# Moving the convolution of nine of 32 feature chunks from TensorE to GpSimd in a fused attention and gated-convolution kernel

## The chip, the cores and the metric

The kernel runs on one core of a Trainium2 chip. The metric is the device time of one execution in microseconds (us). Every run also has a granted TensorE clock, as a share of full speed, and a state: "slow" is a run more than 1.5% above the fastest run of the same kernel. One run of a kernel has no known state.

## The reference, cut to what matters

Attention over sorted blocks (omitted here) gives `x` of 4 batches x 768 positions x 512. The part that the change touches is the gated layer after it:

```python
h = np.maximum(x @ w_in, 0.0)              # 768 x 1024 per batch
hp = zero-padded h, one position at each end
for k in range(3):
    conv_out += conv_w[k][None, None, :] * hp[:, k:k + S, :]   # each feature by itself
gate = 1.0 / (1.0 + np.exp(-conv_out))
return (h * gate @ w_out).astype(np.float32)
```

The 1024 features are eight chunks of 128, one feature per partition; with four batches there are 32 chunks. A chunk's convolution is three taps, each with one weight per feature.

## The kernel before

The program is a list of tokens, `ORDER`, and each token issues a few instructions. All engines take their own instructions in the order in which the tokens stand, so the table is the schedule. A digit after `d` is one of four PSUM slots; a last `a` or `d` chooses ScalarE or VectorE for an eviction.

```python
NET, NHE, NSG, NXN, NOS = 6, 12, 6, 4, 6      # NOS: output buffers
ORDER = """
... S.1.4d3 C.0.5d1 V.1.2d2 R.2.1 E.1.4 K.2.1d0 Ce.0.5 Ve.1.2d H.0.1.1d3 R.2.7 PV.1.3d2 Ge.0.5 ...
"""                                            # cut: 551 tokens in all

def do_R(b, n, eng, slot):                     # GpSimd: one of eight copies for batch b's values
    nc.gpsimd.tensor_copy(rv[:, n * 8:(n + 1) * 8, 0:CC], vr[b]...)

def do_H / do_He                               # cut: first layer on TensorE; hE = 0.5 * relu, bf16

def do_C(b, f, eng, slot):                     # convolution of chunk f on TensorE
    pu = bank(slot, [128, 2, 512])
    def mm(n, x0, nx, tap, src, start=False, stop=False):
        for i in range(2):                     # diagonal 64 x 64 weights, two quadrants
            o = 64 * (1 - i if n else i)
            nc.tensor.matmul(pu[o:o + 64, n, ...], lhsT=dg[64 * i:64 * (i + 1), tap, f, :],
                             rhs=src[64 * i:64 * (i + 1)], ..., tile_position=(64 * i, o))
    mm(...)                                    # eight calls, 16 matmuls

def do_Ce(b, f, eng, slot):                    # ScalarE: tanh of the sum, three instructions
    nc.scalar.activation(sg[:, 0:384], pu[:, 0, 0:384], AF.Tanh)
    for o in (0, 64):
        nc.scalar.activation(sg[o:o + 64, 384:768], pu[64 - o:128 - o, 1, 0:384], AF.Tanh)

def do_Ge(b, f, eng, slot):                    # VectorE: the gate product, hg = (sg + 1) * hE
    nc.vector.scalar_tensor_tensor(out=hg, in0=sg, scalar=1.0, in1=hx[:, :, 0:128],
                                   op0=OP.add, op1=OP.mult)

def do_O / do_Oe                               # cut: second layer, eviction to o_sb{x % NOS}, store
```

The convolution is a product with diagonal weights, so TensorE spends 16 matmuls on work that is one multiply per element and tap. GpSimd is used for loads, for a few set-up products and for the `rv` copies (`do_R`), on which the `V` matmuls of the next batch wait.

The softmax here doesn't subtract the row's maximum and nothing guards it: scores larger than these inputs give would overflow.

## Time and profile before

| | before |
|---|---|
| median of 3 runs | 178.96 us (178.92 to 181.91) |
| TensorE busy, profiled run | 162.9 of 176.1 us (92%), clock 1.0 |
| TensorE weight loads busy | 106.9 us (61%) |
| GpSimd busy | 42.0 us (24%) |
| the 32 gate products on VectorE | 981 ns each |

The lines themselves are in the prediction below, but for that of the gate product:

```profile
L495 DVE SCALAR_TENSOR_TENSOR hg<-sg,hE 128x768 bf16<-128x768 bf16 x32 | 30.8, 981 | 2.7 <-ACT sg L486 2.5
```

A slice digit is the busy share of a fortieth of the span in tenths; the chain's shares say whose work, followed back from the last instruction, the end rested on. In a group line, `x32 | 30.8, 981` is the count, the busy us in all and the mean ns of one; after the next bar come the idle us just before them and what ended them.

### The profile page before, as it was taken

The page shows a single profiled execution, that of the slowest core. Times are in us where ns is not written, and L with a number is a line of the kernel's source. Part 1 is how long each engine was busy: PE and PEld are TensorE (multiplying, and loading weights), DVE is VectorE, ACT ScalarE, POOL GpSimd, SP SyncE. Part 2 cuts the span into 40 slices and gives each one's busy share as a digit, 9 for nine tenths or more (in the row PEclk, how much of TensorE's full clock was granted, in tenths as well). Part 3 has the DMA queues.
Part 4 walks back from the last instruction along what each step waited for, and adds up shares of the span by engine and source line. Part 5 has one row for each costly group of instructions (what it writes and reads, how often), then busy time and mean ns, then how long its engine had stood idle before and what let it go on. Part 6 is the DMA issues. An engine that isn't in the chain of part 4 may idle for free.

```text
span 176.1 us, 6511 instructions
## 1 busy us (share of the span) xinstructions
PE 162.9 (92%) x2907; PEld 106.9 (61%) x2918; DVE 118.4 (67%) x224; ACT 116.7 (66%) x210; POOL 42.0 (24%) x96
## 2 busy tenths in 40 slices
PE   3997989998889999999999999999999999999991
...
POOL 7850940399791001008600000000000000000000
...
GB/s 48 200 212 89 113 219 217 196 220 209 215 200 218 203 110 4 0 7 0 63 60 120 121 92 90 62 61 4 2 4 60 6 0 0 63 119 60 180 181 119
DMA packets 10688, 18.27 MB, mean 104 GB/s; under 512 B 908, under 2 KB 6052, under 8 KB 10660
## 3 DMA queue, kind: packets, MB, share of 16 engines
...
## 4 chain that ended last, share of the span: by engine, by line
PE 69%; ACT 13%; DVE 10%; issue 3%; DMA 3%; DVEq 0%; ACTq 0%
PE D L502 22%; PE D L447 22%; PE D L467 9%; ACT et L402 4%; PE D L413 4%; PE D L333 3%; PE D L367 3%; DVE hE L457 3%; PE D L430 2%; ACT kT L102 2%; ACT hE L455 2%; DMA sn<-in_sort_net_dram 2%; PE D L394 2%; PE D L230 2%; ACT sg L486 2%
## 5 line engine op out<-in xcount | busy, mean ns | idle before, releaser
L447 PE MATMUL D<-xT,w_in_bf 128*128 128x384 bf16 x256 | 46.3, 326 | 0.8 <-DVE hE L457 0.5
L502 PE MATMUL D<-w_out_bf,hg 128*128 128x512 bf16 x181 | 42.7, 379 | 0.6 <-issue 0.2
L447 PEld LDWEIGHTS <-w_in_bf 128*128 128x128 bf16 x256 | 23.6, 98 | 15.4 <-issue 1.3
L495 DVE SCALAR_TENSOR_TENSOR hg<-sg,hE 128x768 bf16<-128x768 bf16 x32 | 30.8, 981 | 2.7 <-ACT sg L486 2.5
L486 ACT ACTIVATE sg<-D 64x384 bf16<-64x384 f32 x64 | 31.1, 486 | 0.8
L502 PEld LDWEIGHTS <-hg 128*128 128x128 bf16 x192 | 17.8, 98 | 20.6 <-issue 0.8
L354 POOL COPY rv<-vr 128x384 bf16<-128x384 bf16 x24 | 20.9, 910 | 36.6 <-PE D L367 25.6
L402 ACT ACTIVATE et<-D 128x768 bf16<-128x768 f32 x32 | 24.3, 820 | 6.6 <-PE D L394 6.6
L457 DVE TENSOR_SCALAR hE<-D 128x384 bf16<-128x384 f32 x29 | 15.7, 554 | 16.2 <-ACT hE L455 9.7
L455 ACT ACTIVATE hE<-D 128x384 bf16<-128x384 f32 x35 | 16.1, 491 | 14.6 <-PE D L447 7.7
L422 DVE TENSOR_TENSOR xn<-D,rc 96x512 bf16<-96x512 f32 x32 | 22.0, 687 | 1.1
L467 PE MATMUL D<-hE,dg 64*64 64x384 bf16 (+2 forms) x512 | 19.6, 286 | 0.7 <-PE D L394 0.5
L484 ACT ACTIVATE sg<-D 128x384 bf16<-128x384 f32 x32 | 15.8, 492 | 4.2 <-PE D L467 3.4
L106 DVE COPY o_sb<-D 128x512 f32<-128x512 f32 x13 | 8.9, 692 | 13.6 <-PE D L502 11.0
L467 PEld LDWEIGHTS <-dg 64*64 64x64 bf16 x512 | 12.5, 106 | 6.6 <-issue 3.6
L102 ACT COPY o_sb<-D 128x512 f32<-128x512 f32 x11 | 6.4, 587 | 13.8 <-PE D L502 13.7
L413 PE MATMUL D<-vE,et 128*128 128x65 bf16 x256 | 13.2, 194 | 0.8 <-ACT hE L455 0.5
L413 PEld LDWEIGHTS <-et 128*128 128x128 bf16 x256 | 10.6, 98 | 4.2 <-issue 2.2
L102 ACT CAST kT<-D 128x1024 bf16<-128x1024 f32 x10 | 9.9, 1013 | 3.5 <-PE D L333 3.3
L394 PE MATMUL D<-qT,kT 64*128 64x96 bf16 x256 | 9.5, 204 | 1.2 <-DVE qT L106 0.3
L420 DVE RECIPROCAL rc<-D 96x8 f32<-96x8 f32 x32 | 6.3, 198 | 6.0 <-PE D L413 5.9
L430 PE MATMUL D<-ident,xn 96*128 96x96 bf16 x128 | 9.9, 206 | 0.3
...
## 6 DMA issues: line engine op xcount, KB each, us to landing
...
w_out_bf<-in_moe_w_out_dram POOLq DMA_DIRECT2D x1, 1024.0 KB, 12.5
...
sn<-in_sort_net_dram SPq DMA_DIRECT2D x1, 8.0 KB, 3.2
```

The lines of the kernel that those rows point to most:

```text
L102: nc.scalar.copy(dst, src)
L354: nc.gpsimd.tensor_copy(rv[:, n * 8:(n + 1) * 8, 0:CC], vr[b].rearrange("p c d -> p d c")[:, n * 8:(n + 1) * 8, :])
L402: nc.scalar.activation(et[:, 0:8 * BLK].rearrange("c (h q) -> c h q", h=2), at.pop(("S", b, j))[:, :, 0:4 * BLK], AF.Exp, scale=scale)
L413: nc.tensor.matmul(pov[:, hh, ii, :], lhsT=et[:, o:o + 128], rhs=vE[b % 2][:, (hh * HP + hp) * NB + sub * 4 + ii, 0:65], start=True, stop= ...
L422: nc.vector.tensor_mul(xn.rearrange("c i h d -> c h i d"), pov[0:BLK, :, :, 0:64], rc.unsqueeze(3).to_broadcast((BLK, 2, 4, D)))
L447: nc.tensor.matmul(ph[:, n, 0:384], lhsT=w_in_bf[:, kc, f * 128:(f + 1) * 128], rhs=xT[(b, s)][:, kc, :], start=(kc == 0), stop=(kc == KC ...
L455: nc.scalar.activation(hv, src, AF.Relu, scale=0.5)
L457: nc.vector.tensor_scalar(hv, in0=src, scalar1=0.0, scalar2=0.5, op0=OP.max, op1=OP.mult)
L467: nc.tensor.matmul(pu[o:o + 64, n, (x0 - 3 * n) * 128:(x0 - 3 * n + nx) * 128], lhsT=dg[64 * i:64 * (i + 1), tap, f, :], rhs=src[64 * i:64 ...
L486: nc.scalar.activation(sg[o:o + 64, 384:768], pu[64 - o:128 - o, 1, 0:384], AF.Tanh)
L495: nc.vector.scalar_tensor_tensor(out=hg.rearrange("p (x c) -> p x c", c=128), in0=sg.rearrange("p (x c) -> p x c", c=128), scalar=1.0, in1 ...
L502: nc.tensor.matmul(po, lhsT=hgs[(b, f)][:, x * 128:(x + 1) * 128], rhs=w_out_bf[:, f, :], start=(f == 0), stop=(f == FC - 1))
```

## The change

Its intent is to take nine convolutions from the nearly full TensorE and to do them on the nearly idle GpSimd, as scaled copies and adds in SBUF with an fp32 sum. ScalarE then needs one tanh instead of three. Two output buffers are given up, presumably for the fp32 tiles, and a new table is used for the whole kernel.

```diff
-NET, NHE, NSG, NXN, NOS = 6, 12, 6, 4, 6
+NET, NHE, NSG, NXN, NOS = 6, 12, 6, 4, 4
+ON_POOL = [(0, 1), (0, 3), (1, 1), (1, 3), (1, 5), (2, 1), (2, 3), (2, 5), (3, 1)]
 ORDER = """
-Q.0.1d0 K.0.2d1 K.0.1d2 Qe.0.1d Ke.0.2a M.0.2d1 ...
+K.0.2d0 Ke.0.2a Q.0.1d1 Qe.0.1d K.0.1d2 bdm.0d3 ...          # cut: the whole table is new
+... C.0.5d3 S.1.5d0 U.0.1.0 PV.1.0d1 Ce.0.5 ... He.0.3.1d U.0.1.1 ...
 """
+    def do_U(b, f, half, eng, slot):
+        g = b * FC + f
+        h = hE[g % NHE]
+        hx = h[:, 2:].rearrange("p (x c) -> p x c", c=130)
+        if half == 0:
+            at[("C", b, f)] = moep.tile([128, NX, 128], FP, name="u", bufs=2)
+            nc.gpsimd.tensor_scalar(at[("C", b, f)], in0=hx[:, :, 0:128], scalar1=cws[:, 1, f:f + 1],
+                                    scalar2=None, op0=OP.mult)
+        u = at[("C", b, f)]
+        a = moep.tile([128, 2 + NX * 130], FP, name="tap", bufs=1)
+        nc.gpsimd.tensor_scalar(a, in0=h, scalar1=cws[:, 2 * half, f:f + 1], scalar2=None, op0=OP.mult)
+        ...                                    # cut: parts = the shifted views of a, 640 and 128 wide
+        for x0, nx, src in parts:
+            nc.gpsimd.tensor_tensor(out=u[:, x0:x0 + nx], in0=u[:, x0:x0 + nx], in1=src, op=OP.add)
     def do_Ce(b, f, eng, slot):
+        if (b, f) in ON_POOL:
+            nc.scalar.activation(sg, pu.rearrange("p x c -> p (x c)"), AF.Tanh)
+            return
```

So a chunk on GpSimd is three scaled copies (one of 768 and two of 782 elements) and four adds (two of 640, two of 128). Below, "chunk" means these seven instructions.

More of the change, by code (lines that the diff above doesn't have):

```diff
@@ L13 @@
 AX = mybir.AxisListType
-NET, NHE, NSG, NXN, NOS = 6, 12, 6, 4, 6
+NET, NHE, NSG, NXN, NOS = 6, 12, 6, 4, 4
+ON_POOL = [(0, 1), (0, 3), (1, 1), (1, 3), (1, 5), (2, 1), (2, 3), (2, 5), (3, 1)]
 SUBS = [(hp, s) for s in range(2) for hp in range(4)]
 ORDER = """
-Q.0.1d0 K.0.2d1 K.0.1d2 Qe.0.1d Ke.0.2a M.0.2d1 M.0.1d0 win.0 M.0.0d3 Ke.0.1d lk.1 bdm.0d2 Me.0.2a Me.0.0a K.0.0d1
-lv.1 lq.1 lk.2 Ke.0.0a Me.0.1d lv.2 bdv.0 V.0.0d0 V.0.1d2 S.0.0d3 S.0.1d1 dg.0.2 Ve.0.0d E.0.0 Ve.0.1d V.0.3d0
-S.0.2d2 E.0.1 V.0.2d3 E.0.2 S.0.3d1 Ve.0.3d S.0.5d0 bd.1 Ve.0.2d bd.3 E.0.3 PV.0.0d3 X.0.0 E.0.5 S.0.6d2 PV.0.1d1
@@ L24 @@
-S.0.7d0 X.0.1 PV.0.2d3 lq.2 E.0.6 T.0.0d2 S.0.4d1 E.0.7 Te.0.0a PV.0.3d0 E.0.4 X.0.2 T.0.1d3 bd.2 PV.0.5d2 Te.0.1a
-T.0.2d1 X.0.3 Te.0.2d T.0.3d0 Te.0.3d PV.0.4d3 X.0.5 PV.0.6d1 H.0.0.0d0 R.1.7 H.0.2.0d2 X.0.4 K.1.1d3 He.0.1.0a
-He.0.0.0d He.0.5.0d He.0.4.0a K.1.2d0 Ke.1.2a X.0.6 Ke.1.1d K.1.0d2 H.0.3.0d1 lk.3 T.0.4d3 Ke.1.0a R.1.1 R.1.6
-T.0.5d0 Te.0.4d PV.0.7d2 R.1.0 He.0.7.0d H.0.1.0d3 He.0.6.0a R.1.2 R.1.3 X.0.7 dg.0.1 T.0.6d1 Te.0.5d He.0.2.0a
-He.0.3.0d Te.0.6d V.1.3d2 V.1.0d0 Ve.1.0a Q.1.1d1 Ve.1.3d Q.1.0d3 lq.3 R.1.5 T.0.7d0 Qe.1.1d Te.0.7a S.1.3d1 Qe.1.0d
@@ L29 @@
-E.1.3 S.1.2d2 dg.0.0 S.1.0d3 E.1.2 S.1.1d0 H.0.2.1d1 S.1.5d2 E.1.1 V.1.1d0 R.1.4 E.1.0 He.0.5.1d He.0.4.1d E.1.5
-Ve.1.1d S.1.4d3 C.0.5d1 V.1.2d2 R.2.1 E.1.4 K.2.1d0 Ce.0.5 Ve.1.2d H.0.1.1d3 R.2.7 PV.1.3d2 Ge.0.5 PV.1.1d1 Ke.2.1a
-X.1.3 He.0.2.1a R.2.0 X.1.1 C.0.2d0 R.2.3 He.0.3.1a H.0.0.1d3 PV.1.0d1 Ce.0.2 T.1.3d2 He.0.0.1d X.1.0 He.0.1.1a
-S.1.7d0 PV.1.2d3 Te.1.3a C.0.1d2 E.1.7 T.1.0d1 Ce.0.1 PV.1.7d0 Te.1.0a X.1.2 H.0.3.1d3 X.1.7 He.0.7.1d He.0.6.1a
-T.1.2d0 Te.1.2d S.1.6d2 E.1.6 Ge.0.1 C.0.3d1 T.1.1d3 PV.1.5d0 Q.2.0d2 Te.1.1a X.1.5 R.2.2 R.2.6 K.2.2d3 Ce.0.3
@@ L34 @@
-Ke.2.2a Q.2.1d0 Qe.2.0d C.0.0d1 C.0.7d2 PV.1.6d3 Qe.2.1d Ce.0.0 H.1.0.0d0 X.1.6 Ce.0.7 T.1.7d1 Te.1.7a H.1.1.0d3
-He.1.0.0d Q.3.1d2 Q.3.0d1 Ge.0.2 He.1.2.0a He.1.3.0a Ge.0.3 He.1.1.0a Qe.3.1d K.2.0d3 T.1.6d0 R.2.5 Ge.0.0 Ke.2.0a
-lv.3 R.2.4 H.1.3.0d2 He.1.7.0a PV.1.4d3 He.1.6.0a Te.1.6d V.2.2d0 Qe.3.0d C.0.4d1 T.1.5d2 X.1.4 H.1.2.0d3 Ve.2.2d
-Ce.0.4 T.1.4d0 Te.1.5d S.2.1d2 C.0.6d1 He.1.4.0d He.1.5.0a S.2.3d3 E.2.1 Te.1.4d K.3.1d0 Ge.0.7 Ce.0.6 E.2.3 wout.0
-H.1.2.1d2 Ke.3.1d S.2.0d1 S.2.2d0 He.1.5.1d E.2.0 H.1.0.1d3 E.2.2 K.3.0d1 He.1.1.1a He.1.4.1d Ge.0.6 He.1.0.1d
@@ L39 @@
-V.2.0d0 V.2.3d3 Ke.3.0a C.1.4d2 Ve.2.3a Ge.0.4 Ce.1.4 Ve.2.0d H.1.1.1d1 K.3.2d3 He.1.3.1a He.1.2.1d V.2.1d0 S.2.4d2
-H.1.3.1d1 Ke.3.2d He.1.7.1d C.1.1d3 E.2.4 Ve.2.1a He.1.6.1a Ce.1.1 C.1.0d2 PV.2.3d0 Ge.1.4 O.0.4d1 Ce.1.0 C.1.5d3
-X.2.3 C.1.3d0 Oe.0.4d Ce.1.5 PV.2.1d1 R.3.5 O.0.1d2 C.1.2d3 Ge.1.1 Ce.1.3 Ce.1.2 X.2.1 Oe.0.1d Ge.1.5 C.1.7d1
-PV.2.0d2 O.0.3d0 X.2.0 O.0.2d2 Ge.1.2 Ce.1.7 Oe.0.3d S.2.5d0 R.3.2 E.2.5 Ge.1.0 S.3.1d1 R.3.4 R.3.3 Oe.0.2d C.1.6d3
-E.3.1 O.0.0d2 Ge.1.3 Ce.1.6 T.2.3d1 Ge.1.7 O.0.5d0 Oe.0.0d R.3.7 Ge.1.6 Te.2.3a PV.2.2d1 R.3.1 T.2.0d2 Oe.0.5a X.2.2
@@ L44 @@
-Te.2.0a O.1.0d3 T.2.1d1 T.2.2d2 V.3.1d0 Oe.1.0a Te.2.2d R.3.0 S.2.7d3 S.2.6d2 Te.2.1a Ve.3.1a O.1.2d1 R.3.6 E.2.6
-O.1.3d0 Oe.1.2d PV.2.4d1 E.2.7 Oe.1.3a V.3.2d3 Ve.3.2a X.2.4 V.3.3d2 PV.2.6d0 X.2.6 H.2.1.0d1 T.2.4d3 Te.2.4d
-Ve.3.3a PV.2.5d0 S.3.4d2 X.2.5 He.2.3.0a V.3.0d3 He.2.2.0a Ve.3.0d S.3.0d1 E.3.4 PV.2.7d0 E.3.0 O.1.5d2 T.2.6d3
-T.2.5d1 X.2.7 Oe.1.5d H.2.0.0d0 Te.2.5d S.3.3d1 S.3.2d2 E.3.2 Te.2.6d O.1.1d3 E.3.3 He.2.0.0a He.2.1.0d T.2.7d2
-Te.2.7d PV.3.0d1 Oe.1.1a S.3.6d0 X.3.0 E.3.6 PV.3.1d2 H.2.1.1d3 S.3.5d0 S.3.7d1 X.3.1 PV.3.3d2 He.2.3.1a E.3.5
@@ L49 @@
-He.2.2.1d H.2.2.1d3 X.3.3 PV.3.2d2 T.3.1d0 E.3.7 H.2.2.0d1 He.2.5.1a X.3.2 Te.3.1a T.3.2d2 He.2.4.1d Te.3.2d T.3.0d0
-C.2.3d3 Te.3.0d PV.3.6d2 T.3.3d0 X.3.6 He.2.5.0a He.2.4.0a Te.3.3d H.2.0.1d1 Ce.2.3 T.3.6d2 He.2.1.1a PV.3.7d0
-He.2.0.1d C.2.5d3 Te.3.6a X.3.7 C.2.2d1 PV.3.5d2 Ce.2.5 H.2.3.0d0 X.3.5 He.2.6.0d C.2.0d2 He.2.7.0d Ce.2.2 C.2.1d3
-PV.3.4d1 Ce.2.0 Ge.2.3 Ge.2.2 O.1.4d0 H.3.1.0d2 X.3.4 Ce.2.1 Oe.1.4a T.3.4d3 T.3.7d0 Ge.2.0 Te.3.4d He.3.3.0d
-He.3.2.0a H.3.0.0d1 H.2.3.1d2 T.3.5d3 Te.3.7d Ge.2.1 He.3.1.0a Te.3.5d H.3.2.0d0 C.2.4d3 He.3.0.0d He.2.6.1a
@@ L54 @@
-He.2.7.1d He.3.4.0d C.2.6d2 He.3.5.0d Ce.2.4 C.2.7d1 H.3.3.1d0 Ce.2.6 H.3.0.1d3 H.3.3.0d2 Ce.2.7 H.3.1.1d1 Ge.2.5
-He.3.7.1d He.3.0.1a He.3.1.1d Ge.2.4 He.3.6.1a He.3.6.0a He.3.7.0a He.3.2.1a Ge.2.7 He.3.3.1a H.3.2.1d0 Ge.2.6
-C.3.1d1 C.3.2d2 O.2.4d3 He.3.5.1a Ce.3.1 Ce.3.2 C.3.3d1 He.3.4.1d C.3.0d0 Oe.2.4a C.3.5d2 O.2.3d3 Ge.3.1 Ge.3.2
-Ce.3.3 Oe.2.3d O.2.0d1 Ce.3.0 Ce.3.5 C.3.4d3 C.3.7d0 Ge.3.0 Ce.3.4 Oe.2.0d C.3.6d2 Ge.3.3 Ge.3.4 Ce.3.6 O.2.2d1
-Ge.3.5 Ge.3.6 Ce.3.7 Ge.3.7 O.2.5d3 O.2.1d2 Oe.2.5a O.3.1d3 Oe.2.1d O.3.4d2 Oe.2.2a O.3.0d1 O.3.5d0 Oe.3.1d O.3.3d3
@@ L59 @@
-Oe.3.4d Oe.3.0a Oe.3.5a O.3.2d0 Oe.3.3d Oe.3.2a
+K.0.2d0 Ke.0.2a Q.0.1d1 Qe.0.1d K.0.1d2 bdm.0d3 bdv.0 K.0.0d1 Ke.0.0d win.0 M.0.1d0 M.0.0d3 Ke.0.1a Me.0.0d M.0.2d2
+lk.1 Me.0.1a lv.1 lq.1 lv.2 Me.0.2a S.0.0d0 E.0.0 lk.2 S.0.3d2 V.0.0d3 V.0.1d0 V.0.2d1 Ve.0.0d E.0.3 V.0.3d2 Ve.0.2d
+S.0.2d3 Ve.0.1a S.0.5d0 S.0.1d1 Ve.0.3d PV.0.3d2 E.0.2 E.0.1 PV.0.2d3 S.0.4d1 X.0.3 E.0.5 PV.0.0d2 E.0.4 S.0.6d0
+X.0.2 PV.0.1d1 T.0.2d3 dg.0.1 dg.0.0 X.0.0 E.0.6 X.0.1 bd.1 T.0.0d2 PV.0.4d0 Te.0.2a T.0.3d3 T.0.1d1 X.0.4 Te.0.0a
@@ new lines @@
+Te.0.3a Te.0.1a PV.0.6d2 S.0.7d3 bd.2 E.0.7 PV.0.5d0 H.0.3.0d1 lq.2 K.1.1d3 X.0.6 He.0.6.0a Ke.1.1a K.1.2d2 X.0.5
+Ke.1.2a H.0.0.0d0 He.0.1.0a He.0.7.0a K.1.0d3 He.0.0.0d R.1.6 R.1.2 PV.0.7d2 X.0.7 lk.3 H.0.2.0d0 T.0.6d1 R.1.3
+R.1.7 He.0.4.0a H.0.1.0d2 R.1.5 Ke.1.0d He.0.3.0a T.0.7d3 Te.0.6d T.0.4d1 He.0.5.0d R.1.1 V.1.1d0 R.1.0 Te.0.7d
+T.0.5d3 He.0.2.0d V.1.3d2 Ve.1.1a Te.0.4d Te.0.5d Q.1.1d1 R.1.4 Qe.1.1d Q.1.0d0 V.1.0d3 Ve.1.3a Qe.1.0a S.1.2d1
+E.1.2 lq.3 dg.0.2 H.0.0.1d2 S.1.3d0 S.1.1d1 Ve.1.0d H.0.2.1d3 He.0.1.1d He.0.5.1d E.1.3 E.1.1 S.1.4d0 V.1.2d1
@@ new lines @@
+He.0.4.1d R.2.6 Ve.1.2d He.0.0.1a E.1.4 S.1.0d2 E.1.0 C.0.5d3 S.1.5d0 U.0.1.0 PV.1.0d1 Ce.0.5 X.1.0 H.0.1.1d2 E.1.5
+He.0.2.1a He.0.3.1d U.0.1.1 T.1.0d1 S.1.6d3 PV.1.2d0 bd.3 Te.1.0d PV.1.1d2 R.2.2 C.0.0d1 E.1.6 U.0.3.0 X.1.2 Ce.0.1
+U.0.3.1 C.0.2d3 R.2.1 X.1.1 R.2.3 PV.1.4d0 Ce.0.0 Ce.0.2 Q.2.0d1 R.2.0 H.0.3.1d2 X.1.4 T.1.1d3 He.0.7.1a Ge.0.1
+PV.1.3d0 Qe.2.0d K.2.1d1 R.2.5 He.0.6.1d Te.1.1a T.1.2d2 X.1.3 PV.1.5d3 R.2.4 Ke.2.1a Te.1.2d S.1.7d0 X.1.5 K.2.2d2
+PV.1.6d1 T.1.3d3 E.1.7 Ke.2.2a Te.1.3a X.1.6 Q.2.1d0 T.1.5d1 Qe.2.1d Ge.0.0 C.0.4d2 PV.1.7d3 Te.1.5a T.1.4d1 Te.1.4d
@@ new lines @@
+H.1.1.0d0 Ce.0.3 X.1.7 C.0.6d1 He.1.3.0d Ce.0.4 Q.3.1d2 Ge.0.2 R.2.7 He.1.2.0a Ce.0.6 V.2.1d0 Q.3.0d3 Qe.3.1d
+Qe.3.0d Ve.2.1a K.2.0d1 H.1.0.0d2 He.1.1.0d T.1.6d3 T.1.7d0 Ke.2.0a Te.1.6d He.1.0.0a V.2.2d1 V.2.0d2 Te.1.7a
+K.3.2d0 K.3.1d3 Ve.2.0d Ke.3.1d lv.3 Ve.2.2a C.0.7d1 H.1.2.1d2 Ke.3.2a S.2.2d3 Ce.0.7 Ge.0.3 S.2.3d0 wout.0
+He.1.5.1d He.1.4.1a H.1.0.1d1 S.2.0d2 He.1.1.1d E.2.2 Ge.0.6 E.2.3 S.2.1d3 V.2.3d0 He.1.0.1a R.3.5 E.2.0 E.2.1
+Ge.0.7 K.3.0d1 U.1.1.0 H.1.2.0d2 Ke.3.0a Ge.0.4 He.1.4.0a R.3.0 Ve.2.3a H.1.3.1d3 He.1.5.0d C.1.0d2 R.3.6 C.1.4d1
@@ new lines @@
+PV.2.1d0 U.1.1.1 He.1.6.1a He.1.7.1d Ge.0.5 H.1.1.1d3 R.3.4 Ce.1.0 X.2.1 PV.2.2d2 He.1.2.1d H.1.3.0d0 Ce.1.4
+He.1.3.1d PV.2.3d3 X.2.2 O.0.4d1 He.1.6.0d S.3.1d2 X.2.3 PV.2.0d3 Ce.1.1 R.3.2 He.1.7.0a Oe.0.4d S.2.6d0 E.3.1
+C.1.2d1 X.2.0 U.1.5.0 E.2.6 S.2.5d2 U.1.3.0 R.3.7 Ge.1.1 Ce.1.2 T.2.0d3 Te.2.0d O.0.0d0 T.2.1d1 E.2.5 Te.2.1d
+T.2.2d3 C.1.7d2 S.2.4d1 Oe.0.0a PV.2.6d0 R.3.3 U.1.5.1 Te.2.2d Ce.1.7 Ge.1.0 O.0.3d3 T.2.3d2 E.2.4 X.2.6 V.3.2d0
+Te.2.3a C.1.6d1 Oe.0.3d Ve.3.2d PV.2.4d3 Ce.1.6 O.0.1d2 PV.2.5d1 Oe.0.1a R.3.1 S.2.7d0 E.2.7 X.2.4 S.3.0d3 E.3.0
@@ new lines @@
+V.3.1d2 Ge.1.4 X.2.5 V.3.0d1 Ve.3.1d V.3.3d0 O.0.2d3 Ge.1.2 U.1.3.1 PV.2.7d2 Ve.3.0a T.2.4d1 Ve.3.3a Ge.1.6 Te.2.4a
+X.2.7 H.2.1.0d0 T.2.5d2 Oe.0.2a PV.3.0d1 Ce.1.5 H.2.0.0d3 Te.2.5a He.2.3.0a He.2.2.0d Ce.1.3 T.2.7d2 Te.2.7a X.3.0
+T.2.6d0 Te.2.6a He.2.0.0d O.0.5d1 T.3.0d0 Oe.0.5a Ge.1.7 H.2.1.1d2 Te.3.0a S.3.5d0 He.2.2.1a S.3.3d1 He.2.1.0d
+S.3.2d3 Ge.1.3 He.2.3.1d H.2.0.1d2 E.3.3 E.3.5 PV.3.3d1 Ge.1.5 O.1.2d0 E.3.2 Oe.1.2a X.3.3 He.2.0.1a PV.3.1d1
+O.1.1d3 He.2.1.1a PV.3.2d2 S.3.7d0 Oe.1.1a E.3.7 X.3.1 C.2.2d1 X.3.2 C.2.0d3 T.3.2d2 Te.3.2d Ce.2.2 O.1.5d0 Ce.2.0
```

20 lines of the change are left out of this document (19 added, 1 removed).

## The prediction

> **What bounds the kernel now.** I read the page first: busy shares, slices, chain shares.
>
> ```profile
> PE 162.9 (92%) x2907; PEld 106.9 (61%) x2918; DVE 118.4 (67%) x224; ACT 116.7 (66%) x210; POOL 42.0 (24%) x96
> ...
> PE   3997989998889999999999999999999999999991
> ...
> POOL 7850940399791001008600000000000000000000
> ...
> PE 69%; ACT 13%; DVE 10%; issue 3%; DMA 3%; DVEq 0%; ACTq 0%
> ```
>
> TensorE is nearly full from the second slice to the last but one, 69% of the chain that ended last is its work, and GpSimd is idle from the 21st slice (88 us) on. So the kernel is bound by TensorE, and GpSimd has room, most of it late. Next, what the convolution takes of TensorE: the windows view over everything, for its line L467 alone (column after the window: PE busy), then the chain of waits in order of time near the end (start, length, work).
>
> ```profile
> 0.00:180.00 180.00, 19.61 (x512) 12.48 (x512) 0.99 0.46 101
> ```
> ```profile
> 146.84 1.11 PE D L467 x32
> ...
> 149.78 1.60 PE D L467 x48
> ...
> 151.76 3.19 PE D L502 x14
> ```
>
> The groups view gives that line 19.6 + 9.0 + 7.4 = 36.0 us, but its matmuls run side by side; of the clock they cover 19.61 us. One chunk is 16 matmuls, so 32 chunks cost 0.61 us each. The chain agrees: two chunks 1.11 us, three 1.60 us, so 0.49 us for one more and about 0.13 us each time PE turns to this form. One chunk alone costs 0.6 to 0.7.
>
> Third, where a wait ends: by the windows of 20 us PE is busy 19.7 of 20 at 120 to 140 and at 140 to 160, ScalarE 18.8 of 20 at 140 to 160. That late stage has two nearly full engines; VectorE has 12.5.
>
> **What the Trainium skill says.** (1) "TensorEngine Tiling (Array Packing)", Key Properties: tiles of the array run in parallel, and a change of the tiling mode drains the engine. The trace agrees: 36.0 us of matmuls in 19.61 us, and the 0.13 us per turn. (2) "GPSIMD Engine Reference", section 3: a two-input add of 2048 fp32 took 4497 ns on GpSimd, about twice VectorE. The trace has 1062 ns for 512 (below), a little less per element. (3) "SBUF — State Buffer", Who interferes with whom: a VectorE instruction with two SBUF inputs and a GpSimd instruction that reads SBUF exclude each other for the whole instruction. The gate product L495 is such a one, and the timeline shows it where `rv` copies run beside it:
>
> ```profile
> 83.28 3.17 POOL L354 COPY rv<-vr 128x384 bf16<-128x384 bf16 x3
> ```
> ```profile
> 82.72 1.43 DVE L495 SCALAR_TENSOR_TENSOR hg<-sg,hE 128x768 bf16<-128x768 bf16 x1
> ...
> 86.05 1.21 DVE L495 SCALAR_TENSOR_TENSOR hg<-sg,hE 128x768 bf16<-128x768 bf16 x1
> ...
> 89.25 0.95 DVE L495 SCALAR_TENSOR_TENSOR hg<-sg,hE 128x768 bf16<-128x768 bf16 x1
> ```
>
> The product takes 0.95 us undisturbed and 1.43 and 1.21 us here; the copies take 1.06 us each where their median is 0.85.
>
> **The change part by part.** *Removed from PE:* nine of 32 chunks, 9 x 0.61 = 5.5 us, all inside the saturated stretch. This is the ceiling of the gain, 3.1% of 178.96, unless the new table packs better.
>
> *Removed from ScalarE:* a chunk's three tanh calls (492 + 2 x 486 = 1464 ns) become one of 768 elements. The exponential of the same size takes 820 ns. 0.64 us each, 5.8 us in all, 2.6 us of it (four chunks) late, where ScalarE is nearly full. A conv also held one of the four PSUM slots from its first matmul to its last tanh, 0.6 + 1.5 = 2.1 us; nine of these go.
>
> *Added on GpSimd:* per chunk a scaled copy of 768, two of 782, two adds of 640 and two of 128, all into fp32. The nearest rows:
>
> ```profile
> L298 POOL TENSOR_TENSOR dg<-cws,m 128x512 bf16<-128x512 f32 x3 | 3.2, 1062 | 0.0
> ...
> L317 POOL TENSOR_TENSOR bd<-mask,pt 128x128 bf16<-128x128 f32 x3 | 1.2, 439 | 0.0
> ...
> L159 POOL TENSOR_SCALAR_AFFINE_SELECT sel<-sel 32x512 bf16<-32x512 bf16 x1 | 0.6, 628 | 0.1
> ...
> L171 POOL TENSOR_TENSOR gm<-gm,gm 128x2 f32<-128x2 f32 x1 | 0.2, 198 | 0.1
> ...
> L164 POOL TENSOR_SCALAR_AFFINE_SELECT gm<-gm 128x2 f32<-128x2 f32 x1 | 0.2, 189 | 0.1
> ```
>
> Two inputs: 0.20 us plus (1062 - 198) / 510 = 1.7 ns an element, so 640 cost 1.28 us and 128 cost 0.44. One input: 0.19 us plus (628 - 189) / 510 = 0.86 ns, so 768 cost 0.85 and 782 cost 0.86. No row is a scaled copy; that the select stands for it is my choice. Dependent GpSimd instructions follow each other 0.07 us apart (the start-up selects). First half: 0.85 + 0.86 + 1.28 + 0.44 + 4 x 0.07 = 3.7 us. Second: 0.86 + 1.28 + 0.44 + 0.21 = 2.8. A chunk is 6.5 us, nine are 58 us. GpSimd goes from 42 to about 100 of 171 us, and its delay is no longer hidden everywhere.
>
> *Where it lies.* I added one duration per PE token along the new table (first-layer pair 1.40, output 1.75, conv 0.56, scores 0.36, values 0.43, K, M and V 0.64 to 0.70), counting from its first token. The sum is 162.6 us against 167.6 for the old table: 5.0 less, all of it convolutions. With GpSimd's instructions in their order:
> - batch 1: the seventh of the eight copies that the V tokens of batch 3 need (R.3.1, read by V.3.0) ends at about 87.4, and V.3.0 stands at 87.7. Slack 0.3 us. The last conv half ends at 90.2; its tanh stands at 93.6.
> - batch 2: the second layer's input He.2.1.1 at 105.8 frees the first; the halves end at 116.5 and 119.3, their tanh stand at 115.8 and 119.3. No slack.
> - batch 3: ends at 139.1, tanh at 139.4. No slack.
>
> So the table fits my GpSimd durations almost exactly; whoever made it used about the same ones. If they hold, PE waits little; every longer instruction goes straight to a tanh at the head of ScalarE's queue, which holds back the evictions behind it.
>
> *Contention.* Some 63 GpSimd instructions meet the 32 gate products (VectorE in them 31 of about 125 us, a fifth to a quarter). At a quarter and half a product lost, 63 x 0.25 x 0.48 = 7.5 us are added to the 58, 0.8 us a chunk.
>
> *Moved:* four instead of six output buffers. A buffer is busy 0.69 (eviction) + 2.0 (transfer) = 2.7 us, and in the tail the closest reuse is two outputs, 3.5 us. Free. The prologue starts with K.0.2 before Q.0.1: the queries no longer fill the wait for the mix matrix, but the first scores can come about 1 us earlier. I count it as zero.
>
> Sum: -5.5 (PE), -0.5 (ScalarE and PSUM relief late), +1.6 (late tanh in batches 2 and 3 through contention, about 0.8 each where slack is nil): -4.4 us, 174.6 us.
>
> **The rivals.** (a) *GpSimd's scaled copy is slow.* At the rate of the strided `rv` copy, (854 - 190) / 384 = 1.7 ns an element, each costs 1.5 us, a chunk 8.5. Then R.3.1 and V.3.0 slip by some 3 us and the tanh of batch 2 by some 4, part of which PE takes up elsewhere: 176 to 179 us, "same". For it: no row shows this form. Against: `rv` reads with a stride and this does not; the table's spacing suits 6.5. (b) *The shared SBUF path makes VectorE the limit.* Products of 0.95 stretched to 1.5 us would add 10 us to its 118; it frees PSUM, so PE would stop. For: the 1.43 above. Against: VectorE has a third of its time free. About 177 to 181. (c) *ScalarE and PSUM were what kept PE from packing*, and the gain exceeds the matmuls removed: 171 to 173. For: 18.8 of 20 late. Against: PE has only 0.5 us of idle between 120 and 160 to win.
>
> **Range and chances.** A gain over 2% needs 175.4 or less, that is 3.6 of the 5.5 us kept; my centre keeps 4.4. The main spread is GpSimd's duration (6.5 to 8.5 us a chunk) and what PE hides of it, so it runs upward: 171.0 to 179.5. Faster 0.52, same 0.37, slower 0.11.
>
> **What would show it.** PE busy on the convolution line near 19.61 x 23/32 = 14.1 us; the conv halves start to start at 3.7 and 2.8 us; GpSimd busy 95 to 108 us; ScalarE busy near 111; few new waits of tanh on GpSimd, and of V on `rv`. Wrong if the scaled copies exceed 1.2 us, if gate products average over 1.2 us, or if PE's idle time between 40 and 160 us grows by more than 3 us, naming `rv` or ScalarE.

## The result, and the profile after

| | before | after |
|---|---|---|
| median | 179.08 us, 4 runs (178.92 to 181.91) | 215.89 us, 4 runs (213.94 to 220.0) |
| granted clock of the fast runs | about 1.0 | 0.926 to 0.933 |

The ratio is 1.2023, with a 95% interval of 1.1916 to 1.2131: the change is 20% slower, and the time lies far above the range. A ratio here is the mean time of one kernel's fast runs over that of the other's fast runs of the same rounds, so it is not quite the ratio of the medians. All outputs were correct.

The profiled run of the changed kernel was a slow one (span 218.1 us, clock 0.896; the fast ones are 2% shorter), so its durations are read for their kind and place, and the size of the loss is taken from the timed runs. These are the lines of its page that answer to the first ones of before, with the clock row added:

```profile
PE 170.7 (78%) x2761; PEld 111.0 (51%) x2774; DVE 117.2 (54%) x215; ACT 117.0 (54%) x201; POOL 141.4 (65%) x159
...
PE   4986689999379796992995098899639829999792
...
POOL 7908502879999951899999960079999999300000
PEclk9999589999958999997698579999957967999999
...
POOL 43%; PE 33%; DVE 9%; issue 6%; ACT 6%; DMA 2%; POOLq 0%; ACTq 0%; DVEq 0%
```

The row of TensorE now has holes in its middle, where GpSimd's row is full. The chain has turned over: 43% of it is GpSimd's and 33% TensorE's. The clock row drops to 5 to 7 in slices in which TensorE stands or in the one after.

The next lines are groups of instructions of the changed kernel, from its page (L519 the gate product, L493 and L489 the scaled copies, L500 the adds, L507 the new tanh), and two of its waits (what waited, for what: us in all, times, longest):

```profile
L519 DVE SCALAR_TENSOR_TENSOR hg<-sg,hE 128x768 bf16<-128x768 bf16 x32 | 35.8, 1140 | 12.1 <-ACT sg L507 7.7
L493 POOL TENSOR_SCALAR tap<-hE,cws 128x782 f32<-128x782 bf16 x18 | 40.4, 2244 | 0.6
L500 POOL TENSOR_TENSOR u<-u,tap 128x640 f32<-128x640 f32 (+1 forms) x36 | 37.5, 1063 | 1.5
...
L489 POOL TENSOR_SCALAR u<-hE,cws 128x768 f32<-128x768 bf16 x9 | 22.6, 2513 | 16.0 <-ACT hE L457 14.2
...
L507 ACT ACTIVATE sg<-u 128x768 bf16<-128x768 f32 x9 | 7.6, 846 | 28.1 <-POOL u L500 28.1
```
```profile
ACT sg L507 <- POOL u L500: 28.1, 6, 7.9
...
PE D L369 <- POOL rv L356: 7.4, 2, 5.0
```

A scaled copy takes 2.24 us (L493) or 2.51 (L489) on average where the prediction put 0.86. Six of the nine new tanh calls wait for GpSimd, 28.1 us in all, and hold ScalarE's queue meanwhile. The `V` matmuls (L369) wait for `rv` copies, which stand in the same GpSimd queue behind the chunks.

The chain of the changed kernel in order of time shows one chunk on the path (start, length, work), 10.6 us from 48.52 to 59.17:

```profile
48.52 2.21 POOL u L489
50.73 2.26 POOL tap L493
53.06 1.83 POOL u L500 x2
54.98 2.26 POOL tap L493
57.31 1.86 POOL u L500 x2
```

The intended saving is there too. The windows view over everything for the convolution line of the changed kernel (second number after the window: TensorE busy):

```profile
0.00:220.00 220.00, 14.51 (x368) 8.96 (x368) 0.89 0.38 83
```

It was 19.61 us, so 5.1 us of TensorE's work went, at a lower clock than before. The questions are what the GpSimd work itself costs, what its collisions cost, and why so much of its delay reached the end.

### The profile page after: what moved, and what is told of

Its sections match the earlier page's. It is cut to its first block, busy times and chain, and to the rows that moved or that the text cites. A ratio compares the mean times of both kernels' runs of the same rounds, so it can differ in the third digit from the quotient of the medians.

```text
span 218.1 us, 6275 instructions
## 1 busy us (share of the span) xinstructions
PE 170.7 (78%) x2761; PEld 111.0 (51%) x2774; DVE 117.2 (54%) x215; ACT 117.0 (54%) x201; POOL 141.4 (65%) x159
## 4 chain that ended last, share of the span: by engine, by line
POOL 43%; PE 33%; DVE 9%; issue 6%; ACT 6%; DMA 2%; POOLq 0%; ACTq 0%; DVEq 0%
POOL tap L493 15%; POOL u L500 14%; PE D L526 10%; POOL u L489 9%; PE D L449 7%; POOL rv L356 3%; PE D L220 3%; DVE hE L459 2%; PE D L232 2%; DVE hg L519 2%; DMA out_dram<-o_sb 2%; PE D L369 2%; ACT kT L104 2%; PE D L362 2%; DVE xn L424 2%
## 5 line engine op out<-in xcount | busy, mean ns | idle before, releaser
L449 PE MATMUL D<-xT,w_in_bf 128*128 128x384 bf16 x256 | 49.7, 344 | 5.5 <-ACT sg L511 4.8
L526 PE MATMUL D<-w_out_bf,hg 128*128 128x512 bf16 x179 | 46.8, 402 | 3.3 <-ACT o_sb L104 1.4
L519 DVE SCALAR_TENSOR_TENSOR hg<-sg,hE 128x768 bf16<-128x768 bf16 x32 | 35.8, 1140 | 12.1 <-ACT sg L507 7.7
L493 POOL TENSOR_SCALAR tap<-hE,cws 128x782 f32<-128x782 bf16 x18 | 40.4, 2244 | 0.6
L500 POOL TENSOR_TENSOR u<-u,tap 128x640 f32<-128x640 f32 (+1 forms) x36 | 37.5, 1063 | 1.5
L489 POOL TENSOR_SCALAR u<-hE,cws 128x768 f32<-128x768 bf16 x9 | 22.6, 2513 | 16.0 <-ACT hE L457 14.2
L507 ACT ACTIVATE sg<-u 128x768 bf16<-128x768 f32 x9 | 7.6, 846 | 28.1 <-POOL u L500 28.1
L511 ACT ACTIVATE sg<-D 64x384 bf16<-64x384 f32 x46 | 22.3, 485 | 0.5
L457 ACT ACTIVATE hE<-D 128x384 bf16<-128x384 f32 x29 | 13.5, 492 | 12.2 <-PE D L449 7.7
L396 PE MATMUL D<-qT,kT 64*128 64x96 bf16 x256 | 10.6, 217 | 9.9 <-issue 5.1
L369 PE MATMUL D<-bd,rv 128*64 128x64 bf16 x384 | 9.5, 206 | 7.9 <-POOL rv L356 7.4
L432 PE MATMUL D<-ident,xn 96*128 96x96 bf16 x128 | 10.7, 215 | 5.8 <-ACT o_sb L104 5.4
L469 PE MATMUL D<-hE,dg 64*64 64x384 bf16 (+2 forms) x368 | 14.5, 293 | 0.0
```

The source lines that it names most:

```text
L449: nc.tensor.matmul(ph[:, n, 0:384], lhsT=w_in_bf[:, kc, f * 128:(f + 1) * 128], rhs=xT[(b, s)][:, kc, :], start=(kc == 0), stop=(kc == KC ...
L489: nc.gpsimd.tensor_scalar(at[("C", b, f)], in0=hx[:, :, 0:128], scalar1=cws[:, 1, f:f + 1], scalar2=None, op0=OP.mult)
L493: nc.gpsimd.tensor_scalar(a, in0=h, scalar1=cws[:, 2 * half, f:f + 1], scalar2=None, op0=OP.mult)
L500: nc.gpsimd.tensor_tensor(out=u[:, x0:x0 + nx], in0=u[:, x0:x0 + nx], in1=src, op=OP.add)
L519: nc.vector.scalar_tensor_tensor(out=hg.rearrange("p (x c) -> p x c", c=128), in0=sg.rearrange("p (x c) -> p x c", c=128), scalar=1.0, in1 ...
L526: nc.tensor.matmul(po, lhsT=hgs[(b, f)][:, x * 128:(x + 1) * 128], rhs=w_out_bf[:, f, :], start=(f == 0), stop=(f == FC - 1))
```

## The experiments

Two theories were set against each other. **Theory A:** the scaled copy is slow by itself, and the late chunks hold back ScalarE and the `V` matmuls. **Theory B:** GpSimd's reads and VectorE's gate products exclude each other, and this collision is what stretches both. A third suspect was the new table. Ten kernels ran. Those that give a wrong result (e3, e4, e5, e8, e9, e10) still passed the comparison, because an error in a few gates stays within its tolerance. They are tools to measure with, not candidates.

### e1: the instructions by themselves

The kernel before, with two rounds of GpSimd instructions on scratch tiles behind its last `rv` copy, where GpSimd is idle.

```diff
-NET, NHE, NSG, NXN, NOS = 6, 12, 6, 4, 6
+NET, NHE, NSG, NXN, NOS = 6, 12, 6, 4, 3
+    for _ in range(2):
+        nc.gpsimd.tensor_scalar(pf, in0=pb, scalar1=w, scalar2=None, op0=OP.mult)                     # 782
+        nc.gpsimd.tensor_scalar(pf[:, 0:256], in0=pb[:, 0:256], scalar1=w, scalar2=None, op0=OP.mult)
+        ...                                                # cut: constant scalar, bf16 out, fp32 in
+        nc.gpsimd.tensor_copy(pf[:, 0:F], pb[:, 0:F])                                                 # F = 768
+        nc.gpsimd.tensor_tensor(out=pf[:, 0:F], in0=pb[:, 0:F], in1=w.to_broadcast((128, F)), op=OP.mult)
+        nc.gpsimd.tensor_tensor(out=pf[:, 0:640], in0=pg[:, 0:640], in1=pg[:, 2:642], op=OP.add)
```

> The kernel before, with two rounds of nine GpSimd instructions on scratch tiles behind its last rv copy (three output buffers instead of six). It measures the disputed cost by itself. Theory A (the scaled copy is slow by itself): the 782-wide one with a scalar per partition takes about 2.2 us here too, with the slope of 2.6 to 2.9 ns an element between 256 and 782. Theory B (it is slow in the changed kernel only because it shares the SBUF path or reads a busy tile): about 0.9 us here. Open: whether a constant scalar, a bf16 output, an fp32 input, a plain cast or a product with a broadcast scalar is cheaper. Time within 1% of before, as GpSimd is idle there.

From the timeline of this kernel, GpSimd alone, second round (start, length, instruction):

```profile
107.86 2.26 POOL L528 TENSOR_SCALAR p_out<-p_src,cws 128x782 f32<-128x782 bf16 x1
110.21 0.93 POOL L529 TENSOR_SCALAR p_out<-p_src,cws 128x256 f32<-128x256 bf16 x1
...
117.78 0.83 POOL L533 CAST p_out<-p_src 128x768 f32<-128x768 bf16 x1
118.69 1.47 POOL L534 TENSOR_TENSOR p_out<-p_src,cws 128x768 f32<-128x768 bf16 x1
120.24 1.25 POOL L535 TENSOR_TENSOR p_out<-p_two 128x640 f32<-128x640 f32 x1
```

The kernel took 182.76 us in its one run; only the durations are used. The scaled copy takes 2.26 us by itself, the same as in the changed kernel. From 256 to 782 elements it grows by (2.26 - 0.93) / 526 = 2.5 ns an element. It is not the fp32 output: with bf16 out it took 2.20 us. Nor is it the scalar taken from a tile: with a constant it took 2.13 (2.71 in the first round). A plain copy of 768 elements takes 0.83 us, which is what the prediction had assumed, and a two-input product with the weight broadcast takes 1.47, less than the one-input scaled copy. The add of 640 took 1.25, as predicted (1.28). So the *size* of a chunk is Theory A's: by these times it is 3 x 2.26 + the adds' 2 x 1.83 (the chain above) + gaps = some 10.6 us.

### e2: the new table with all convolutions on TensorE

```diff
-ON_POOL = [(0, 1), (0, 3), ...]
+ON_POOL = []
 # table: each "U.b.f.0 U.b.f.1" taken out, "C.b.f" put back in a free PSUM slot near "Ce.b.f";
 # some of these "Ce" tokens stand elsewhere too
```

> The new order table and four output buffers, but all 32 convolutions on TensorE: the nine GpSimd chunks are dropped and nine conv tokens set into free PSUM slots near their tanh. Theory A (GpSimd's duration made the 37 us): 177 to 184 us, because PE has the work of the kernel before in a table that was not made for it. Rival C (the new table, with its other prologue, or the four buffers are bad): 195 us or more. The 3 us in which PE stood still near 21 us shows here as well if the prologue of the table is its cause.

The median was 198.9 us, with one fast run (193.0), so there is no ratio. By its expectation this would have spoken for the table as the cause. It does not decide that: the inserted convolutions took PSUM slots that the table had not planned for, probably the reason for the loss, and e4 below shows that the table itself is not that slow. A table and its set of convolutions belong together; only the reverse, taking work away, can be read.

### e3: chunks of the predicted length, with their reads

The same seven instructions per chunk in the same places, but the scaled copies are 256 wide (0.93 us each), so a chunk is 3 x 0.93 + 2 x 1.83 + gaps = about 6.6 us, as the prediction had it.

```diff
-        nc.gpsimd.tensor_scalar(a, in0=h, scalar1=cws[:, 2 * half, f:f + 1], scalar2=None, op0=OP.mult)
+        nc.gpsimd.tensor_scalar(a[:, 0:256], in0=h[:, 0:256], scalar1=cws[:, 2 * half, f:f + 1], scalar2=None, op0=OP.mult)
 # and the centre tap on two of six blocks; u and tap as constant tiles, filled once
```

> The changed kernel with scaled copies of 256 columns instead of 768 and 782 (wrong result on purpose), so that one takes about the 0.86 us that the prediction gave it; everything else as in the change. Theory A (the scaled copy is the one mis-sized term): 172 to 179 us, near the predicted 174.6, GpSimd busy near 105 us. Rival C (table) or rival D (the shared SBUF path and VectorE): 185 us or more.

The median was 191.89 us, the ratio 1.0683 (1.0579 to 1.0787). The expected 172 to 179 was missed: with the durations that the prediction had assumed, the change is still 7% *slower*. Length explains about two thirds of the loss (1.2023 to 1.0683), but it is not the only fault. The timeline of this kernel shows the other, VectorE's gate products beside GpSimd's adds:

```profile
102.59 2.58 POOL L506 TENSOR_TENSOR us<-us,tap 128x640 f32<-128x640 f32 x2
103.28 2.70 DVE L525 SCALAR_TENSOR_TENSOR hg<-sg,hE 128x768 bf16<-128x768 bf16 x2
```

Two adds that take 1.83 us undisturbed take 2.58, and two products that take 1.9 take 2.70.

### e4: the new table with GpSimd's work almost nothing

Each half becomes one product of two columns, so the tokens, the order and the tanh stay.

```diff
+        nc.gpsimd.tensor_scalar(u[:, half, 0:2], in0=h[:, 2:4], scalar1=cws[:, 1, f:f + 1], scalar2=None, op0=OP.mult)
 # in place of the scaled copies and adds
```

> The changed kernel with each half of a GpSimd chunk cut to one 2-column product (wrong result on purpose): the table, the buffers and ScalarE's part of the change stay, GpSimd's time almost goes. Theory A2 (what is left of the loss in e3, about 11 us, is GpSimd being late through contention, not the table): 172 to 178 us. Rival C (the table alone is that bad, as e2 suggests): 184 us or more.

The median was 177.79 us, the ratio 0.9866 (0.9765 to 0.9967). This is what the new table and the nine convolutions less on TensorE are worth *if GpSimd's work cost nothing*: 1.3%, not 3.1%. ScalarE is not relieved: it is busy 116.7 us here as in the kernel before, because the new table hands it nine evictions that VectorE had (83 against 74 in `ORDER`). The convolution line is at 14.02 us here (the prediction said 14.1). The 5.6 us taken off TensorE came through by less than half. Its profiled run (178.41 us, the slowest of its three fast ones) shows two places where the rest can have gone. In the first 40 us TensorE is busy 31.8 us here and 34.5 us in the kernel before, 2.7 us less. And in the tail the evictions wait for output buffers, and TensorE for them:

```profile
ACT o_sb L104 <- DMA out_dram<-o_sb: 8.9, 2, 6.6
...
PE D L520 <- ACT o_sb L104: 1.4, 1, 1.4
```

With four buffers, outputs 0 and 4 of a batch share one, and in this table three evictions close together want it (`Oe.2.0d`, `Oe.2.4d`, `Oe.3.4a`): the chain of e4 runs through two stores of 2.0 us (from 159.56 and 162.40 us) before TensorE goes on at 165.71. Of the kernel before, the waits view lists no output matmul that waits for an eviction.

### e5: chunks of the predicted length that read almost nothing

As e4, plus memsets of about 0.74 us, five in the first half and four in the second. A chunk is again near the predicted length (6.9 us), but the memsets only write; what still reads is the product of two columns in each half (9.0 us of the 69.2 below).

```diff
+NFILL = (5, 4)
+        for n in range(NFILL[half]):
+            nc.gpsimd.memset(u if n % 2 == 0 else tap0, 0.0)
```

> As e3, but a half is one 2-column product and five or four memsets of about 0.72 us (3.8 and 3.1 us, so 6.9 us a chunk against 6.6 in e3), which write SBUF and read nothing (wrong result on purpose). Theory D2 (in e3 the exclusion between GpSimd's reads and the two-input gate products lengthens both and pushes GpSimd's chain): gate products back near 0.95 us where they ran 1.1, GpSimd's chunks undisturbed, and 4 us or more faster than e3, so 183 to 187. Theory A2 without contention: same as e3 within 2 us, 189 to 192.

The median was 181.05 us, but two of the four runs were slow; the ratio of the fast ones is 0.9997 (0.9912 to 1.0083). The gain was larger than expected. e3 and e5 differ in whether the chunk reads SBUF, hardly in how long GpSimd is at work on chunks: 68.4 us in e3 and 69.2 us in e5 (sums of their group lines). Gate product and chain shares, from the pages of e3 and then of e5:

```profile
PE 42%; POOL 27%; DVE 12%; ACT 10%; issue 4%; DMA 2%; POOLq 0%; ACTq 0%; DVEq 0%
...
L525 DVE SCALAR_TENSOR_TENSOR hg<-sg,hE 128x768 bf16<-128x768 bf16 x32 | 33.9, 1078 | 2.7 <-ACT sg L517 2.7
```
```profile
PE 67%; DVE 14%; ACT 9%; DMA 4%; issue 4%; ACTq 0%; DVEq 0%
...
L516 DVE SCALAR_TENSOR_TENSOR hg<-sg,hE 128x768 bf16<-128x768 bf16 x32 | 30.5, 973 | 2.4 <-ACT sg L508 2.3
```

Without reads the product is back at 973 ns, GpSimd has no share of the chain, and no tanh waits for GpSimd. With reads GpSimd has 27%, the tanh calls wait 10.4 us for it, and the `V` matmuls 5.0 us. So e3 lies 6.9 points of the ratio, some 12 us, above e5, and most of this is Theory B's part. Not all of it need be: the memsets write `u` and `tap` in turn, and the last one of a chunk writes `tap`, so the tanh is let go one memset before the chunk ends. In e8, which is built alike, a tanh starts at 58.63 us, when the last write of `u` ends, while the last memset runs from 58.54 to 59.29. At the price that length has below (13.4 points for 4.0 us a chunk), these 0.7 us would be some 2.3 points; e5's chunk, by plan 0.3 us longer than e3's, would put some 1 point back. The reads then cost roughly 4.5 to 7 points, 8 to 12 us: an estimate, which no run settles.

### e6: the same arithmetic with broadcast products

Scaled copies replaced by the faster form that e1 found (about 8.2 us a chunk by e1's times). Its result is right.

```diff
-        nc.gpsimd.tensor_scalar(a, in0=h, scalar1=cws[:, 2 * half, f:f + 1], scalar2=None, op0=OP.mult)
+        nc.gpsimd.tensor_tensor(out=a, in0=h, in1=cws[:, 2 * half, f:f + 1].to_broadcast((128, 2 + NX * 130)), op=OP.mult)
```

> The change with its scaled copies written as products with a broadcast scalar, which the probe showed at 1.47 us for 768 instead of 2.2. Correct. A chunk goes from 10.4 to about 8.1 us. If GpSimd's chain sets the time, nine chunks give back between half and all of 9 x 2.3 = 21 us: 196 to 206 us. If GpSimd did not set it, 214 us as before.

The median was 207.51 us, the ratio 1.1518 (1.1408 to 1.1628): 5 points better than the change and still 15% slower than before; its fast runs (206.06 to 208.2) lie just above the expected 196 to 206. In its (slow) profiled run the gate product averages 1299 ns, more than with the longer one-input copies (1140), and a broadcast product 1567 to 1752 ns instead of 1470. All the instructions of a chunk now have two inputs; that they collide with the gate products more for this reason is likely, but not tested.

### e7: a milder version in the old table

Five chunks whose values are ready early and needed late, with broadcast products and the old table; their tanh and gate stand about 10 us later. Its result is right.

```diff
+ON_POOL = [(0, 4), (0, 6), (1, 1), (2, 5), (3, 1)]
 # old table: their C tokens out, U tokens after He, Ce and Ge some 10 us later; tap in bf16; own sg tile;
 # NOS = 4; the load of w_out ("wout.0") moved as well
```

> The table of the kernel before with only five chunks on GpSimd (0.4, 0.6, 1.1, 2.5, 3.1), as broadcast products with a bf16 tap, one after the other in GpSimd's idle stretches, with their tanh and gate product set about 10 us later, still ahead of the outputs that need them. Correct. PE loses 5 x 0.61 = 3.0 us of work. If the mechanism of the change is sound and only its durations and table were wrong: 175.5 to 178 us against 179. If the gate products' contention or the later tanh costs as much as it saves: 179 to 183.

The median was 188.41 us (fast runs 186.17 and 186.43; no ratio was formed, and the kernel before had 179.22 to 181.05). It is slower than before and than either outcome that was expected. On its page 27 of the gate products average 1295 ns.

### e8: chunks of the true length that read almost nothing

As e5 with eight and six memsets, 10.7 us a chunk.

```diff
-NFILL = (5, 4)
+NFILL = (8, 6)
```

> As e5, with eight and six memsets in the halves (6.1 and 4.6 us, 10.7 a chunk), which is the length that the scaled copies and adds of the change have undisturbed (10.4), again without reads of SBUF beyond two columns (wrong result on purpose). It closes the two-by-two of length and reads: short and no reads 181 (e5), short and reads 192 (e3), long and reads 216 (the change). If length and reads add up, 205. If the length alone does little as long as nothing reads, 185 to 192, and the two multiply in the change.

The median was 204.82 us, the ratio 1.1347 (1.1205 to 1.1489), where a sum of separate effects said 205. With e3, e5 and the change itself this makes a table of two by two:

| ratio to before | almost no reads | with reads | reads add (with the earlier tanh) |
|---|---|---|---|
| short chunks (about 6.6 to 6.9 us) | 0.9997 (e5) | 1.0683 (e3) | 6.9 points |
| long chunks (about 10.7 us) | 1.1347 (e8) | 1.2023 (the change) | 6.8 points |
| length adds | 13.5 points | 13.4 points | |

Within the intervals (0.9 to 1.4 points each way in these four) the two causes add up, and each has the same size whether the other is there or not. The two kernels of a column let the tanh go at the same point of a chunk, so the effect of length is clean; that of the reads carries the doubt named at e5. The waits of the new tanh on GpSimd go the same way: none in e5, 10.4 us in e3, 17.3 us in e8 and 28.1 us in the change. The chain of e8, from its page, is held by GpSimd although hardly anything collides (its gate product averages 995 ns):

```profile
PE 45%; POOL 28%; DVE 10%; ACT 7%; issue 5%; DMA 3%; ACTq 0%; DVEq 0%
```

### e9: the same removal from TensorE in the old table

The nine convolutions are taken from TensorE and GpSimd's work is as small as in e4, but the order is that of the kernel before.

```diff
-... C.0.1d2 ...
+... U.0.1.0 U.0.1.1 ...      # likewise for the other eight; do_U and do_Ce as in e4, NOS = 4
```

> The table of the kernel before with the same nine convs taken from PE and their GpSimd part cut to two 2-column products as in e4 (wrong result on purpose). The prediction's step 'minus 5.5 us of PE' without the new table: 173 to 175.5 against 179. If the new table was worth something, this is slower than e4 (177.8); if the new table's prologue costs what e4 misses, this is 2 us or more faster than e4.

The fast runs were 177.6 and 178.71 us, the ratio 0.9958 (0.9894 to 1.0021); two slow runs pull the median to 181.86. The expected 173 to 175.5 was missed. Here nothing was added and the convolution line fell to 14.22 us as computed, yet the time fell by 0.4%. The windows view from 40 to 160 us of the kernel before and then of e9 (after the window: busy us of TensorE, weight loads, VectorE, ScalarE, GpSimd):

```profile
40.00:160.00 120.00, 116.24 (x1954) 74.25 (x1962) 84.95 (x141) 94.31 (x176) 19.55 (x23) 1.00 0.33 76
```
```profile
40.00:160.00 120.00, 113.55 (x1837) 71.66 (x1832) 85.82 (x142) 88.33 (x159) 27.52 (x40) 1.00 0.33 76
```

TensorE does 2.7 us less in the same 120 us: where a convolution left the old table, a gap stayed, presumably because the tokens around it wait for evictions and exponentials. ScalarE was relieved here, from 116.7 to 110.0 us, and that did not shorten the kernel either. ScalarE and VectorE hold a larger share of the chain (16% and 11% by e9's page, 13% and 10% before).

### e10: e7 without its reads

```diff
+        for n in range((6, 4)[half]):
+            nc.gpsimd.memset(u, 0.0)          # in place of e7's products and adds
```

> e7 with each half of its five chunks replaced by a 2-column product and six or four memsets (4.6 and 3.1 us, as long as e7's), no reads of SBUF (wrong result on purpose). If the exclusion of the gate products is what made e7 slower than the kernel before: 175.5 to 178.5, gate products at 0.97 us. If the later tanh and gate product were: 184 or more, as e7.

Three of four runs were slow (median 187.0); the one fast run is 182.55 us, between its two expected ranges. e7's fast runs took 186.17 and 186.43, but the kernel before was slower in e7's rounds too (fast runs 179.22 to 181.05, here 178.63 to 179.2). Against the means of these, e7 is 3.5% slower and e10 2.0%: on that single run the reads cost e7 some 1.4 points, and the larger rest of its loss remains without them. In e10's profiled run, a slow one, 27 of the gate products average 1000 ns and GpSimd has 1% of the chain. The likely rest is the later tanh and gate in e7's own table, but no run isolates it.

## Why the prediction was wrong

Step by step, with the ratios as one account: table and removed work -1.3 points (e4); GpSimd work of the predicted length, writes only, +1.3 (e4 to e5); its reads +6.9 (e5 to e3); the true length +13.4 (e3 to the change). These are differences from one kernel to the next, so their sum must give the +20.2 of the change up to rounding and proves nothing; the test of the account is e8, where the sum of the two effects was forecast (205 us) and came: fast runs of 201.58 and 204.43, a ratio of 1.1347 against 0.9997 + 0.134. The steps come from different rounds on different chips, each against the kernel before of its own rounds, with about one point of uncertainty each.

1. **"One input: 0.19 us plus (628 - 189) / 510 = 0.86 ns, so 768 cost 0.85 and 782 cost 0.86. No row is a scaled copy; that the select stands for it is my choice."** This is the step that failed first and most. A scaled copy measured 2.26 us, a chunk 10.6 us instead of 6.5, GpSimd busy 141 us instead of 95 to 108. This mis-sized term is worth 13.4 points, some 24 us, whether or not anything collides. The adds, which had a row of their own form, were right (1.25 us for 640 against 1.28; a pair 1.83 against 1.28 + 0.44 + 0.07). No row of the page has the form of a scaled copy; the probe e1 gave the number.

2. **"(a) GpSimd's scaled copy is slow ... part of which PE takes up elsewhere: 176 to 179 us".** The rival named the right cause, but gave it 8.5 us a chunk and let TensorE hide most of the delay. e6 has near 8 us a chunk by e1's times (9.4 in its profile) and took 206 to 208 us in its fast runs; e8 shows that length alone, without collisions, costs 13.5 points. The extra chunk time from e3 to the change is 9 x (10.6 - 6.6) = 36 us, and 24 us of it reached the end. The prediction had itself found no slack in batches 2 and 3 and wrote that "every longer instruction goes straight to a tanh at the head of ScalarE's queue"; its own finding should have made the rival's price far higher. The clock was lower too: TensorE's busy time was 170.7 us in the change's profiled run (clock 0.896) and 159.1 us in e4's (0.99) for the same matmuls; what share of the loss this is was not separated.

3. **"At a quarter and half a product lost, 63 x 0.25 x 0.48 = 7.5 us ... +1.6".** The mechanism was right, the size was not: reads cost some 4.5 to 7 points, 8 to 12 us (see e5). The Trainium skill, "SBUF — State Buffer", Who interferes with whom, says that a VectorE instruction with two SBUF inputs contends with a GpSimd instruction that reads SBUF, "not with one that only writes it"; runs agree (product 1078 ns in e3, 973 in e5). The failed part was to count only GpSimd's lost time. In e3 GpSimd spends no longer on chunks than in e5, and the kernel is still 12 us slower: by the traces both engines wait in turn, the gate products (33.9 us against 30.5), the `rv` copies (24.4 against 21.6), and behind them the second layer, the tanh and the `V` matmuls.

4. **"Removed from PE: nine of 32 chunks, 9 x 0.61 = 5.5 us, all inside the saturated stretch."** The amount was right (19.61 to 14.02 in e4, 14.22 in e9). That it would come off the end was not: of a possible 3.1%, e9 gave 0.4% and e4 1.3%. Two nearly full engines and the chain's 23% on ScalarE and VectorE were on the page before the prediction, and were read as a side remark. The Trainium skill, "Perfetto Trace Analysis", Identifying the Most-Contended Engine, calls the busy share of matmuls no good measure of how near TensorE is to its limit, and names the share of peak arithmetic and that of weight loads instead. On the page of the kernel before, matmuls were at 92% and weight loads at 61%. The prediction built on the first. e9 agrees with the page in so far as taking matmuls away did not shorten the kernel in proportion; whether weight loads say what bounds it, no run tests.

5. **"the queries no longer fill the wait for the mix matrix ... I count it as zero."** In e4 TensorE does 2.7 us less in the first 40 us than in the kernel before. 2.0 us of it is a single standstill without a releaser, which kernels with the old table show too (see what is open), so some 0.7 us is left for the new order.

6. **"0.64 us each, 5.8 us in all"** and **"in the tail the closest reuse is two outputs, 3.5 us. Free."** Neither held in the new table. ScalarE was to be busy near 111 us and was busy 117.0 in the change and 116.7 in e4, since nine evictions came over from VectorE. The buffers were not free: with four of them TensorE waits 1.4 us in the tail of e4 and of the change for an eviction that waits for a store. In the old table (e9) four buffers made ScalarE wait 8.2 us, but no output matmul; the new table with six was not run.

7. **Right:** the tanh of 768 elements (846 ns, estimate 820); the adds; that the table fits 6.5-us chunks if they do not collide (e5, with its slightly earlier tanh: GpSimd off the chain, no tanh waits for it); that the tight place for the copies is the `V` of batch 3, the fourth (the matmuls of L369 wait 7.4 us for `rv`). Of the rivals, (b) went the right way: the gate products reached 1140 ns, under the 1.2 us that was to refute the prediction, and already cost more than foreseen. Its sum was off: 32 products longer by 0.55 us are 17.6 us, not 10. (c), a gain beyond the matmuls removed, is out by e4 and e9. Of the three signs of being wrong that the prediction named, two came: the scaled copies over 1.2 us, and TensorE's idle time between 40 and 160 us, 25.8 us in the change's profiled run against 3.8, with waits for `rv` and ScalarE among it.

**What stays open.** TensorE stands still near 20 to 24 us, with "issue" as the only name, in the profiled runs of all the kernels with the new table (0.8 us in e3 to 3.4 us in e8; 3.1 us in the change, 2.0 in e4) and of two with the old one (e1 3.3 us, e10 3.8), but not in those of the kernel before and of e7, and for 0.5 us in e9. Since it comes and goes with the old table, the table alone is not its cause; no run shows what is. How the cost of the reads divides among their waits, and how much of it is the earlier tanh of e5 and e8, is not separated. Why e2 is as slow as it is, and what e7 and e10 lose apart from reads, is only argued. No version that was run beats both kernels: the best time, e4's, belongs to a kernel that leaves out the work.

## What to carry to other kernels

Before moving work to an engine, run the exact form of instruction on it once, in the idle part of the old kernel: here a copy took 0.83 us and the same copy with a factor 2.26 us, and no row of the profile before had that form. Then price the move from the schedule that results, not from the busy time that goes: where the receiving queue also serves others and no slack is left, lateness reaches the end (here 24 of 36 us), and reads of SBUF by both engines at once delayed both here. Look also at what else a new schedule moves: here nine evictions and two output buffers used up gains that had been counted. To separate such causes, replace the work by write-only instructions of the same length; with length and reads each on and off, four kernels gave two effects that add up, and the stand-in should also let the next engine go at the same moment, which it did not here.

## What the Trainium skill lacked or had wrong

- "GPSIMD Engine Reference", section 4.1 (Engine selection), says that one-input operations on GpSimd are "roughly line-rate". A plain copy of 768 elements took 0.83 us, 1.1 ns an element; a copy scaled by a factor of 782 elements took 2.26 us (2.5 ns an element), longer than a two-input product with a broadcast factor (1.47 us for 768). No figure for the scaled form was found on that page.
- "SBUF — State Buffer", Who interferes with whom, is right on who excludes whom (gate product 973 ns beside writes, 1078 beside reads), but gives no figure for what it costs a schedule: some 4.5 to 7 points of the ratio here (an estimate, see e5), at a mean stretch of the product of 11%.
- No page that was read explains the 0.8 to 3.8 us for which TensorE stands near 20 to 24 us without a releaser in most of the profiled runs (none in that of the kernel before).
